# First steps of entries 4 to 7 folded about the middle row, on sixteen 32x32 tiles

## Chip, cores and metric

The kernel runs on one core of one Trainium2 chip. The metric is the time of one execution on the device in microseconds (us); the median of several runs counts. The engines of the core are named as in the profile: PE (TensorE, matmuls), PEld (its weight loads), DVE (VectorE), ACT (ScalarE), POOL (GpSimd) and SP (SyncE, which here only issues DMA transfers).

## What is computed

Eight entries of 3136 rows and 256 channels go through a global filter (a real Fourier transform along the rows, a product with a filter, the inverse), and the 25088 rows that come out go through a two-layer network with a softmax-like activation and a normalization:

```python
X = np.fft.rfft(x, axis=1)
y = np.fft.irfft(X * (filt_r + 1j * filt_i)[None], n=x.shape[1], axis=1)
h = y.reshape(B * S, D) @ w_in                      # 25088 x 256 @ 256 x 1024
e = np.exp(h - h.max(-1, keepdims=True))
solu = h * (e / (e.sum(-1, keepdims=True) + 1e-9))
mu, var = solu.mean(-1, keepdims=True), solu.var(-1, keepdims=True)
out = ((solu - mu) / np.sqrt(var + 1e-6) * g_ln) @ w_out   # 1024 -> 256
```

## The kernel before

**The transform.** 3136 = 49 x 64. An entry is a grid of 49 rows by 64 columns of 256 channels. Its transform has four parts. The *first step* is a 49-point transform down the columns; a *piece* of it takes four columns from the left and the four mirrored ones from the right, so an entry has 8 pieces. The *forward step* (`forward`, pb), the product with the filter (`multiply`, on DVE) and the *inverse step* (`inverse`, pc) work on 7 groups of an entry, "spectra". The *back transform* (`fetch_back`, `back_halves`, py, and `join_halves`, on DVE) has 8 pieces again and writes the rows `y` that the network reads. Between the parts the data go through DRAM: `d1` after the first step, `d2` after the inverse.

**The network.** Rows go in blocks of 128; 196 blocks. Two blocks make a pair, and both matrix products of a pair are done in seven products in place of eight (Strassen's way): `product(j, m)` is the first layer (m, line 799), `project(p, m)` the second (o, line 935). The sums that this needs are GpSimd's: `pair_sums` of `y` (s, line 778) and `project_sums` of the activation (u and solu_t, line 778). DVE evacuates the first layer (`finish`, lines 820 and 823), normalizes (`normalize`, line 845) and transposes (`turn`, line 863); ACT copies (`keep`, line 809), takes exponentials and squares. `regroup` (line 880) is eight transfers a pair on SP's queue, which bring the transposed activation (turn) into the layout of the second layer (solu_t). `deviations` (lines 890 to 893) is three small operations on GpSimd every fourth block.

**Steps.** The order on every engine is written out by hand. `step(k)` runs once for each block k; even and odd steps do different parts of a pair. Work of the transform is hung into steps through lists: `early`, `middle` and `late` (matmuls of the transform and joins at three places in a step; `late` is at its end), `stores`, `loads` (at the end of a step), `differences` and `products` (at its start), `first_parts` and `second_parts` (the product with the filter). In an even step after the tenth, `differences` and `products` are the first things issued; in an odd one they follow `stores`. `PLAN[e]` names for each entry the steps of its 8 pieces of the first step, its 7 spectra and its 8 back pieces. Engines issue in order, so a waiting instruction holds up all that is behind it on its engine, and a waiting transfer all transfers behind it on its queue.

**The first step of entries 2 to 7, before.** For a piece in step t, `fetch_quarters` loads a row buffer on SP's queue with four transfers: partitions 0 to 48 hold two columns and 64 to 112 the other two, each with its mirror columns beside it. In step t DVE takes the difference of columns and mirrors (line 279, into diff), GpSimd the sum in place (line 285), and in `late[t]` four matmuls of 49 rows on 64x64 tiles (line 294, each in two passes) give the four real combinations into two PSUM banks. Two ACT copies (line 299) bring them back into the row buffer, and in step t+1 two transfers of 200 KB on GpSimd's queue store them to `d1` (line 305). The table `wq_t` holds the weights.

**Row buffers.** Pool `r` has four buffers of 128 x 1024 floats. The pieces of the first step and those of the back transform (t4, loaded on GpSimd's queue, line 380) share them. `row_loads` lists all these loads with the step of their use, t; a short planner puts each into `loads[at]`:

```python
at = max(t - 3, earliest, min(row_loads[n - 4][0] + 1, latest)) if n >= 4 else -1
```

A load waits for the buffer that it is given: for a first-step piece until its store to `d1` has landed, for a back piece until its join has read it.

## Time and profile before

| | |
|---|---|
| median of 3 runs | 1569.08 us (1568.96 to 1569.52) |
| the profiled execution | 1569.28 us, span 1567.5 us, TensorE clock 0.996 |
| L935 second layer, busy | 400.2 + 309.6 us |
| L799 first layer, busy | 398.4 + 307.8 us |
| L396 py, L326 pc and pb | 64.7, 55.7 + 54.1 and 47.8 us |
| L294 pa, entries 2 to 7 | 53.5 + 52.9 us (overlapping), 590 ns each |
| L279 difference, L285 sum | 0.69 us (0.67 to 3.32), 1.28 us each |

The span is the time from the first to the last instruction of the profiled execution. Busy times of one engine's groups can overlap, since matmuls are pipelined and tiles of the array run side by side. A row of the timeline gives start, duration, engine, line, operation, what it writes and reads, how many were merged, and in brackets the idle time before it and what ended it. Steps have no marker in the trace; an even step begins with the first L799 matmul behind the last matmul of `late`.

### The profile page before, as it was taken

To read this page: it belongs to the slowest core of one execution; us is meant where nothing else is said; L and a number is where in the kernel's file an instruction comes from. 1 tells how busy PE (TensorE), PEld (TensorE's weight loads), DVE (VectorE), ACT (ScalarE), POOL (GpSimd) and SP (SyncE) were. 2 spreads that over 40 slices of the span, in tenths; PEclk is the share of its full clock that TensorE was granted. 3 is DMA by queue.
4 is the path that set the end of the run, shared out by engine and by line. 5 is a ranking of instruction groups with operands and counts; after the bars stand their busy time and mean duration, and the time that the engine had idled before them with its cause. 6 is when DMAs were issued, how large, how long until landed. Compare 5 with 4: busy or idle time off the path is not lost.

```text
span 1567.5 us, 36719 instructions
## 1 busy us (share of the span) xinstructions
PE 1532.5 (98%) x12844; PEld 1061.7 (68%) x12844; DVE 1254.9 (80%) x2233; ACT 927.9 (59%) x1898; POOL 1157.2 (74%) x1346
## 2 busy tenths in 40 slices
PE   8988999999999999999999999999999999999997
PEld 5633576667666776667766776667776777777777
DVE  4879878897998789878998698877998777776773
ACT  3565655666556656666566655666556666666663
POOL 2578886697879678887779767786766767676665
PEclk9999999999999999999999999999999999999999
DMA  9768788877987689667886588766874545343434
GB/s 246 252 202 226 218 225 220 227 212 207 252 242 204 173 236 254 196 173 192 249 230 190 152 229 247 203 184 176 233 204 119 138 122 135 88 115 102 116 104 118
DMA packets 342256, 298.07 MB, mean 190 GB/s; under 512 B 27915, under 2 KB 311573, under 8 KB 342073
## 3 DMA queue, kind: packets, MB, share of 16 engines
q1 hardware_dynamic: 278872, 175.82, 42.5%
q0 software_dynamic: 29568, 87.33, 18.6%
q10 hardware_dynamic: 33634, 32.58, 7.2%
q8 instruction: 104, 1.70, 0.5%
q14 instruction: 78, 0.64, 0.1%
HBM read 118.02 MB, written 74.84 MB: 123 GB/s over the span
## 4 chain that ended last, share of the span: by engine, by line
PE 59%; DMA 2%; DVE 0%; SPq 0%; issue 0%; POOL 0%; ACT 0%; ACTq 0%; POOLq 0%
PE o L935 26%; PE m L799 26%; PE py L396 2%; PE pc L326 1%; PE pa L294 1%; PE pb L326 1%; DMA solu_t<-turn 1%; DMA x<-in_x_dram 0%; SPq L880 0%; DMA out_dram<-ot 0%; PE o L899 0%; POOL u L778 0%; ACT e L833 0%; DVE h L845 0%; DVE h L820 0%
## 5 line engine op out<-in xcount | busy, mean ns | idle before, releaser
L935 PEld LDWEIGHTS o<-w_out_sb,solu_t 128*128 128x128 f32 x3136 | 381.1, 192 | 47.3 <-issue 43.5
L799 PE MATMUL m<-w_in_sb,s 128*128 128x512 f32 x784 | 398.4, 609 | 5.8 <-ACT h L809 3.3
L935 PE MATMUL o<-w_out_sb,solu_t 128*128 128x128 f32 x3136 | 400.2, 276 | 1.7 <-DVE ot L955 1.6
L935 PEld LDWEIGHTS o<-w_out_sb,u 128*128 128x128 f32 x2352 | 306.4, 191 | 138.3 <-issue 108.6
L799 PE MATMUL m<-w_in_sb,y 128*128 128x512 f32 x588 | 307.8, 607 | 5.6 <-DVE nmax L823 3.8
L935 PE MATMUL o<-w_out_sb,u 128*128 128x128 f32 x2352 | 309.6, 275 | 2.6 <-POOL u L778 1.8
L845 DVE SCALAR_TENSOR_TENSOR h<-e,h 128x1024 f32<-128x1024 f32 x196 | 308.7, 1575 | 0.4 <-ACT e L833 0.4
L951 ACT ACTIVATE ot<-o,rs_t 128x128 f32<-128x128 f32 x392 | 143.6, 367 | 248.2 <-PE o L935 246.1
L809 ACT COPY h<-m 128x512 f32<-128x512 f32 x294 | 173.2, 589 | 195.6 <-PE m L799 191.0
L778 POOL TENSOR_TENSOR u<-solu_t 128x512 f32<-128x512 f32 x98 | 135.0, 1377 | 184.7 <-DMA solu_t<-turn 126.2
L823 DVE CUSTOM_DVE_ANT_0 h<-m,h 128x512 f32<-128x512 f32 x196 | 134.3, 685 | 165.4 <-ACT h L809 103.1
L853 ACT ACTIVATE h<-h,nmu 128x1024 f32<-128x1024 f32 x196 | 225.1, 1148 | 53.4 <-DVE turn L863 53.4
L863 DVE STREAM_TRANSPOSE turn<-h 128x1024 f32<-128x1024 f32 x196 | 243.0, 1240 | 3.8 <-DVE ot L955 0.3
L833 ACT ACTIVATE e<-h,nmax 128x1024 f32<-128x1024 f32 x196 | 225.3, 1149 | 8.1 <-DVE h L845 6.6
L778 POOL TENSOR_TENSOR u<-solu_t,u 128x512 f32<-128x512 f32 x98 | 136.0, 1388 | 94.0 <-PE o L935 93.4
L799 PEld LDWEIGHTS m<-w_in_sb,s 128*128 128x128 f32 x784 | 127.9, 191 | 90.9 <-issue 71.6
L955 DVE SCALAR_TENSOR_TENSOR ot<-o,rs_t,ot 128x128 f32<-128x128 f32 x299 | 103.7, 347 | 97.0 <-ACT ot L951 59.8
L778 POOL TENSOR_TENSOR u<-u,solu_t 128x512 f32<-128x512 f32 x98 | 161.9, 1652 | 15.9 <-PE o L935 9.0
L799 PEld LDWEIGHTS m<-w_in_sb,y 128*128 128x128 f32 x588 | 96.7, 191 | 102.1 <-issue 46.2
L778 POOL TENSOR_TENSOR solu_t<-solu_t,solu_t 128x512 f32<-128x512 f32 x98 | 155.0, 1581 | 0.9
L778 POOL TENSOR_TENSOR s<-y 128x128 f32<-128x128 f32 x196 | 100.2, 511 | 6.1 <-DMA x<-in_x_dram 5.7
L396 PEld LDWEIGHTS py<-wb_t,t 50*64 50x64 f32 x3584 | 57.6, 135 | 42.9 <-issue 18.7
(121 smaller groups left out, 1953.9 us busy)
## 6 DMA issues: line engine op xcount, KB each, us to landing
solu_t<-turn SPq DMA_DIRECT2D x780, 128.0 KB
out_dram<-ot SPq DMA_DIRECT2D x196, 128.0 KB
t<-d POOLq DMA_DIRECT2D x112, 200.0 KB, 6.8
d<-x POOLq DMA_DIRECT2D x100, 200.0 KB, 5.3
t<-d ACTq DMA_DIRECT2D x37, 512.0 KB
f<-f_dram POOLq DMA_DIRECT2D x37, 512.0 KB, 7.6
d<-g POOLq DMA_DIRECT2D x36, 512.0 KB, 5.0
x<-in_x_dram SPq DMA_DIRECT2D x112, 98.0 KB
```

The costliest lines, as they stand in the source:

```text
L396: nc.tensor.matmul(out=views[g][64 * h:64 * h + 64, cb, i, :], lhsT=t4[rows, i, c0:c0 + 64], rhs=wb_t[rows, 0:N1], start=True, stop=True)
L778: nc.gpsimd.tensor_tensor(out=out, in0=in0, in1=in1, op=op)
L799: nc.tensor.matmul(out=ms[j, bank], lhsT=lhsT, rhs=w_in_sb[:, w, :], start=m in (1, 2, 7), stop=True, skip_group_check=True)
L809: nc.scalar.copy(out=h_half(k, i), in_=ms[j, 0])
L823: nc.vector.tensor_tensor_reduce(out=h_half(k, i), in0=ms[j, bank], in1=h_half(*kept), scale=1.0, scalar=sofar, op0=ALU.add, op1=ALU.min, ...
L833: nc.scalar.activation(out=e, in_=hs[k], func=AFT.Exp, bias=nmaxs.pop(k)[:, 1:2], scale=-1.0, accum_out=esums[g][:, i:i + 1])
L845: nc.vector.scalar_tensor_tensor(out=solu, in0=e, scalar=SHRINK, in1=solu, op0=ALU.mult, op1=ALU.mult, accum_out=nmu)
L853: nc.scalar.activation(out=solu, in_=solu, func=AFT.Square, bias=nmu, scale=-float(DFF), accum_out=variances[g][:, i:i + 1])
L863: nc.vector.transpose(out=turns[g][:, :, i, :], in_=solus[k].rearrange("p (f j) -> p f j", j=32))
L935: nc.tensor.matmul(out=pos[p, bank], lhsT=lhs[:, f, :], rhs=w[:, f, :], start=f == 0 and (m in (1, 2, 7) or alone), stop=True, skip_group_ ...
L951: nc.scalar.activation(out=out_half(p, *to)[0], in_=pos[p, 0], func=AFT.Copy, scale=rs)
L955: nc.vector.scalar_tensor_tensor(out=ot, in0=pos[p, bank], scalar=rs, in1=out_half(p, *kept)[0], op0=ALU.mult, op1=ALU.add)
```

## The change

For entries 4 to 7 (`FOLD = 4`) the first step is folded a second time, about the middle row of the 49: sums and differences of row r and row 48 - r leave combinations of 25 rows. The four combinations need weights of 25 x 25, which stand in a new table `wz` of four 32x32 tiles; it is loaded into the buffer of `wq_t` once entry 3 is done. Two pieces are done at once.

- **Loads.** For rows in mirrored order, 256 KB pieces of x are copied from DRAM to DRAM: `turn_rows` (8 steps ahead), then `mirror_rows` twice (7 and 5 steps ahead, the second from what `turn_rows` wrote). `fetch_folded` then loads two row buffers with two transfers each. All seven transfers of a pair of pieces are on SP's queue, in place of eight. The loads go into `row_loads` with t - 1 as their step.
- **Arithmetic.** In steps t-1 and t: `difference_folded` (DVE) and `sum_folded` (GpSimd), each on 128 x 512, then `fold`, four DVE operations on 128 x 256, in `middle`.
- **Matmuls.** In `late[t]`: 16 matmuls of 25 rows on 32x32 tiles, into four PSUM banks: two that first steps and back transforms use, and the two of the forward and inverse steps. Four ACT copies bring them back.
- **Stores.** In step t+1, one transfer of 512 KB for each of the two pieces on GpSimd's queue; `d1` has 32 rows in place of 25 for these entries.
- **Plan.** The pairs of pieces stand in every fourth step, the first five spectra in every fourth step between them (then every second), back pieces in every second. Entry 3's first steps move from 15, 23, 25 ... 35 to 15, 17 ... 29; its spectra are spread too.

```diff
-    ([15, 23, 25, 27, 29, 31, 33, 35], range(38, 52, 2), range(54, 70, 2)),
-    (range(39, 55, 2), range(58, 72, 2), range(76, 92, 2)),
-    (range(63, 79, 2), range(82, 96, 2), range(100, 116, 2)),
-    (range(87, 103, 2), range(106, 120, 2), range(126, 142, 2)),
-    (range(111, 127, 2), range(130, 144, 2), range(150, 166, 2)),
+    (range(15, 31, 2), [32, 36, 40, 44, 48, 50, 52], range(56, 72, 2)),
+    *((range(24 * e - 61, 24 * e - 45, 4), [24 * e - n for n in (40, 36, 32, 28, 24, 22, 20)],
+       range(24 * e - 16, 24 * e, 2)) for e in range(4, 8)),
...
-    ph = 2 * np.pi * (np.outer(n1, s) % N1) / N1
+    ph = 2 * np.pi * (np.outer(n1 - NS + 1, s) % N1) / N1
...
+    wz = np.zeros((32, 4, 32))
+    for a, table in enumerate((w[0], w[1], w[1], -w[0])):
+        wz[:NS, a, :NS] = table[:NS]
+    wz[NS - 1] /= 2
...
-    d1 = [dram.tile([NS, P, C], FP32, name=f"d1_{e}") for e in range(B)]
+    d1 = [dram.tile([NS if e < FOLD else 32, P, C], FP32, name=f"d1_{e}") for e in range(B)]
...
+        def rows_of(self, i, half, mirror):
+            n2 = N2 - 4 * i - 8 if mirror else 4 * i
+            n1, row = ((0, N2 * C), (N1 - 1, -N2 * C))[half]
+            return x[self.e].offset + (n1 * N2 + n2) * C, row
+
+        def turn_rows(self, i, half, dma):
+            at, row = self.rows_of(i, 1, True)
+            self.turned[i, half] = out = dram.tile([4, 32, 2 * C], FP32, name=f"turned_{self.e}_{i}_{half}")
+            dma(out=out, in_=bass.AP(tensor=x.tensor, offset=at, ap=[[2 * C, 4], [row, 32], [1, 2 * C]]))
+
+        def mirror_rows(self, i, half, dma):
+            self.mirrored[i, half] = out = dram.tile([4, 32, 2 * C], FP32, name=f"mirrored_{self.e}_{i}_{half}")
+            if half == 0:
+                at, row = self.rows_of(i, 0, True)
+                rows = bass.AP(tensor=x.tensor, offset=at + 6 * C, ap=[[row, 32], [-2 * C, 4], [1, 2 * C]])
+            else:
+                rows = self.turned.pop((i, half)).rearrange("a r c -> r a c")[:, ::-1, :]
+            dma(out=out.rearrange("a r c -> r a c"), in_=rows)
+
+        def fetch_folded(self, i, mirror, dma):
+            self.xs[i + mirror] = out = self.pools["r"].tile([P, NCH, C], FP32, ..., tag="r")
+            for half in range(2):
+                if mirror:
+                    rows = self.mirrored.pop((i, half)).rearrange("a r c -> (a r) c")
+                else:
+                    at, row = self.rows_of(i, half, False)
+                    rows = bass.AP(tensor=x.tensor, offset=at, ap=[[2 * C, 4], [row, 32], [1, 2 * C]])
+                dma(out=out[:, 2 * half:2 * half + 2, :].rearrange("p n c -> p (n c)"), in_=rows)
+
+        def folded(self, i, n):
+            return [self.xs[i + m].rearrange("p (h n) c -> p h n c", h=2)[:, :, (n, 1 - n)[m]] for m in range(2)]
+
+        def difference_folded(self, i, n):
+            x0, x1 = self.folded(i, n)
+            self.diffs[i + n] = diff = self.pools["diff"].tile([P, 2, C], FP32, ..., tag="diff")
+            nc.vector.tensor_tensor(out=diff, in0=x1, in1=x0, op=ALU.subtract)
+
+        def sum_folded(self, i, n):
+            x0, x1 = self.folded(i, n)
+            nc.gpsimd.tensor_tensor(out=x0, in0=x0, in1=x1, op=ALU.add)
+
+        def fold(self, i, n):
+            (x0, x1), diff = self.folded(i, n), self.diffs.pop(i + n)
+            for out, in0, in1, op in ((x1[:, 0], x0[:, 0], x0[:, 1], ALU.subtract),
+                                      (x0[:, 0], x0[:, 0], x0[:, 1], ALU.add),
+                                      (x1[:, 1], diff[:, 0], diff[:, 1], ALU.subtract),
+                                      (x0[:, 1], diff[:, 0], diff[:, 1], ALU.add)):
+                nc.vector.tensor_tensor(out=out, in0=in0, in1=in1, op=op)
+
+        def first_folded(self, i, pss):
+            for a, (m, half) in enumerate(((0, 0), (1, 1), (1, 0), (0, 1))):
+                data = self.xs[i + m][:, 2 * half:2 * half + 2, :][:, ::1 - 2 * m]
+                for g in range(4):
+                    rows = slice(32 * g, 32 * g + NS)
+                    nc.tensor.matmul(out=pss[g][32 * a:32 * a + 32], lhsT=wq_t[rows, a], rhs=data[rows],
+                                     start=True, stop=True)
+            for g in range(4):
+                nc.scalar.copy(out=self.xs[i + g // 2][:, 2 * (g % 2):2 * (g % 2) + 2, :], in_=pss[g])
+
+        def store_folded(self, i, dma):
+            dma(out=d1[self.e].rearrange("s (a n) c -> a s n c", a=4)[:, :, NCH * i:NCH * i + NCH, :],
+                in_=self.xs.pop(i))
...
+            elif e >= FOLD:
+                for by, job in ((8, lambda dma, sp=sp, i=i: sp.turn_rows(2 * i, 1, dma)),
+                                (7, lambda dma, sp=sp, i=i: sp.mirror_rows(2 * i, 0, dma)),
+                                (5, lambda dma, sp=sp, i=i: sp.mirror_rows(2 * i, 1, dma))):
+                    loads[t - by].append(lambda job=job: job(nc.sync.dma_start))
+                for n in range(2):
+                    row_loads.append((t - 1, t - 2, -1, lambda sp=sp, i=i, n=n: sp.fetch_folded(
+                        2 * i, n, nc.sync.dma_start)))
+                    differences[t - 1 + n].append(lambda sp=sp, i=i, n=n: sp.difference_folded(2 * i, n))
+                    products[t - 1 + n].append(lambda sp=sp, i=i, n=n: sp.sum_folded(2 * i, n))
+                    middle[t - 1 + n].append(lambda sp=sp, i=i, n=n: sp.fold(2 * i, n))
+                    stores[t + 1].append(lambda sp=sp, i=i, n=n, dma=dma: sp.store_folded(2 * i + n, dma))
+                late[t].append(lambda sp=sp, i=i: sp.first_folded(
+                    2 * i, [psum(f"pa_{sp.e}_{i}_{g}") for g in range(2)] + psum_pair(f"pa_{sp.e}_{i}", False)))
...
+        if k == PLAN[FOLD - 1][0][-1] + 1:
+            nc.gpsimd.dma_start(out=wq_t, in_=wz_dram)
```

More of the change, by code (lines that the diff above doesn't have):

```diff
@@ L36 @@
 EARLY = 3
+FOLD = 4
 PLAN = [
@@ L104, in dft_tables @@
     return wf.reshape(NR, NK).astype(f32), wf0.astype(f32), wq.reshape(P, 2, 64).astype(f32), \
+        np.tile(wz, (4, 1, 1)).astype(f32), \
         (-wi0).reshape(P, NR).astype(f32), (-wb).reshape(P, N1).astype(f32), de.astype(f32)
@@ L120 @@
     nc = tc.nc
-    wf_host, wf0_host, wq_host, wi_host, wb_host, de_host = dft_tables()
+    wf_host, wf0_host, wq_host, wz_host, wi_host, wb_host, de_host = dft_tables()
     wf_dram = nc.inline_tensor(wf_host, name="wf_tbl").ap()
@@ L124 @@
     wq_dram = nc.inline_tensor(wq_host, name="wq_tbl").ap()
+    wz_dram = nc.inline_tensor(wz_host, name="wz_tbl").ap()
     wi_dram = nc.inline_tensor(wi_host, name="wi_tbl").ap()
@@ L149 @@
     wf_t = consts.tile([NR, NK], FP32, name="wf_t")
-    wq_t = consts.tile([P, 2, 64], FP32, name="wq_t")
+    wq_t = consts.tile([P, 4, 32], FP32, name="wq_t")
+    wq_halves = wq_t.rearrange("p (j b) i -> p j (b i)", j=2)
     wi_t = consts.tile([P, NR], FP32, name="wi_t")
@@ L219, in __init__ @@
             self.units = [(i, min(2, NP - i)) for i in range(0, NP, 2)]
+            self.turned, self.mirrored = {}, {}
             self.xs, self.t1s, self.t2s, self.fs, self.prods, self.gs, self.des, self.spectra, self.diffs = (
@@ L294, in first_quarters @@
                     nc.tensor.matmul(out=pss[g][64 * j:64 * j + rows],
-                                     lhsT=wq_t[64 * g:64 * g + N1, j, 0:rows],
+                                     lhsT=wq_halves[64 * g:64 * g + N1, j, 0:rows],
                                      rhs=rhs[64 * g:64 * g + N1], start=True, stop=True)
@@ new lines, in fetch_folded @@
+        def fetch_folded(self, i, mirror, dma):
+            self.xs[i + mirror] = out = self.pools["r"].tile([P, NCH, C], FP32, name=f"x_{self.e}_{i + mirror}",
+                                                             tag="r")
+            for half in range(2):
[5 more added lines that the diff above has]
+                dma(out=out[:, 2 * half:2 * half + 2, :].rearrange("p n c -> p (n c)"), in_=rows)
@@ new lines, in folded @@
+        def folded(self, i, n):
+            return [self.xs[i + m].rearrange("p (h n) c -> p h n c", h=2)[:, :, (n, 1 - n)[m]] for m in range(2)]
+        def difference_folded(self, i, n):
+            x0, x1 = self.folded(i, n)
+            self.diffs[i + n] = diff = self.pools["diff"].tile([P, 2, C], FP32, name=f"diff_{self.e}_{i + n}",
+                                                               tag="diff")
+            nc.vector.tensor_tensor(out=diff, in0=x1, in1=x0, op=ALU.subtract)
@@ L581 @@
             load_w_out(n, nc.sync.dma_start)
-        nc.sync.dma_start(out=wq_t, in_=wq_dram)
+        nc.sync.dma_start(out=wq_halves, in_=wq_dram)
         nc.sync.dma_start(out=wb_t[:, 0:N1], in_=wb_dram)
@@ L1043 @@
         at = max(t - 3, earliest, min(row_loads[n - 4][0] + 1, latest)) if n >= 4 else -1
+        import os
+        if os.environ.get('DBG'): print(n, t, at, latest, row_loads[n-4][0])
         assert at < t
```

## Prediction

> **What bounds the kernel now.** I read the page's first, second and fourth part, then the engines by stretch, then the order of instructions on TensorE, GpSimd and VectorE in steps of the stage that changes. Page:
>
> ```profile
> PE 1532.5 (98%) x12844; PEld 1061.7 (68%) x12844; DVE 1254.9 (80%) x2233; ACT 927.9 (59%) x1898; POOL 1157.2 (74%) x1346
> PEclk9999999999999999999999999999999999999999
> PE 59%; DMA 2%; DVE 0%; SPq 0%; issue 0%; POOL 0%; ACT 0%; ACTq 0%; POOLq 0%
> ```
>
> TensorE is busy 98% of the span at full clock, and the chain that ended last is TensorE almost alone. So a matmul taken away is time won, and any wait put in front of TensorE is time lost: it has no idle time to absorb one. By stretch (length, busy time of PE, PEld, DVE, ACT, POOL, clock, DMA share, GB/s):
>
> ```profile
> 740.00:920.00 180.00, 180.00 (x1619) 125.13 (x1621) 151.87 (x267) 109.51 (x227) 142.18 (x167) 1.00 0.75 208
> ```
>
> In this stage VectorE (152 of 180) and GpSimd (142) keep up, with little room. TensorE at the end of step 97 and the start of step 98:
>
> ```profile
> 847.30 1.06 PE L935 MATMUL o<-w_out_sb,solu_t 128*128 128x128 f32 x8
> 848.29 0.65 PE L294 MATMUL pa<-x,wq_t 49*64 49x512 f32 x2
> 848.30 0.64 PE L294 MATMUL pa<-diff,wq_t 49*50 49x512 f32 x2
> 848.77 0.59 PE L294 MATMUL pa<-x,wq_t 49*64 49x512 f32 x1
> 849.29 1.12 PE L799 MATMUL m<-w_in_sb,y 128*128 128x512 f32 x2
> 850.26 1.05 PE L935 MATMUL o<-w_out_sb,u 128*128 128x128 f32 x8
> ```
>
> A piece's first step is four 64x64 tiles, each in two passes: all first passes start within 0.01 us, the second ones 0.47 later, and the next projection 1.00 us after the first start. Eight L935 matmuls elsewhere take 0.89 and two L799 0.86; here they take 0.99 and 0.97. So a piece that stands alone costs 1.00 + 0.10 + 0.11 = 1.21 us. Where it follows an inverse step (770.61, next projection 771.60; the last inverse matmuls start at 770.42 and stream 0.21), that switch is paid already and it costs twice 0.43 = 0.87. GpSimd in steps 86 and 87 (they begin at 755.04 and 763.46):
>
> ```profile
> 756.45 1.28 POOL L778 TENSOR_TENSOR u<-solu_t 128x512 f32<-128x512 f32 x1 [5.19 <-DMA solu_t<-turn]
> 757.82 1.28 POOL L778 TENSOR_TENSOR u<-u,solu_t 128x512 f32<-128x512 f32 x1
> 759.03 0.80 POOL L371 DMA_DIRECT2D d<-g  x1
> 759.86 1.45 POOL L778 TENSOR_TENSOR solu_t<-solu_t,solu_t 128x512 f32<-128x512 f32 x1
> 762.01 1.27 POOL L778 TENSOR_TENSOR u<-solu_t,u 128x512 f32<-128x512 f32 x1 [0.70 <-PE o L935]
> 763.24 0.65 POOL L890 TENSOR_TENSOR rs<-var,floor 128x4 f32<-128x4 f32 x1
> ...
> 765.58 0.80 POOL L713 DMA_DIRECT2D f<-f_dram  x1
> 766.40 1.29 POOL L285 TENSOR_TENSOR x<-x 113x512 f32<-113x512 f32 x1
> ```
>
> The chain is in order: projection sums, store, sums, deviations, filter load, and only then the sum of a piece; 10.5 us from 756.45 to 767.69 without the 0.70 for TensorE. It ends 4.2 us into the odd step, and nothing but that step's last matmuls (6.2 us in) needs it. VectorE in step 97 (842.05 to 849.29) and at the end of step 109 (936.66):
>
> ```profile
> 845.22 1.24 DVE L863 STREAM_TRANSPOSE turn<-h 128x1024 f32<-128x1024 f32 x1
> 846.37 0.71 DVE L820 TENSOR_SCALAR_CACHE_REDUCE h<-m,nmax 128x512 f32<-128x512 f32 x1
> ...
> 936.93 1.22 DVE L845 SCALAR_TENSOR_TENSOR h<-e,h 128x1024 f32<-128x1024 f32 x1
> ```
>
> VectorE's L820 clears the PSUM bank that the projection at 849.29 writes; it ends at 847.08, 2.2 us early. The normalization of an odd step ends 1.5 us inside the next even one (938.15).
>
> **The change, part by part.** *TensorE.* Before, entries 4 to 7 have 32 pieces; by the plan 22 stand in a step with an inverse and 10 alone: 22 x 0.87 + 10 x 1.21 = 31.2 us. After, 16 groups of 16 tiles, all alone, two pieces each. The trace has no 32x32 tile. Bounds: all 16 at once, 1.21 us, or one column of four after another, 4 x 0.87 + 0.34 = 3.8. The four tiles shown run at once, 0.01 to 0.03 apart, so I take 1.21 plus 0.14 for 16 starts: 16 x 1.35 = 21.6, a gain of 9.6. The new plan spreads the spectra over every fourth step: forward steps that share a step with a back transform fall from 27 to 19, each giving up about one switch, 0.34 us: +2.8. With one more shared piece in entry 3, TensorE gains 7.
>
> *VectorE.* The difference stays (0.69, L279's median). Added are four 128x256 operations a piece, 128. Nearest row: L349 on 64x256, 417 ns; 512 wide it is 0.69 to 2.78 when GpSimd runs beside it. I take 1.5 us for the four (bounds 1.4 and 3.3). A pair adds 3 us to two steps in which VectorE was idle 4 to 5 us with a back transform alone: hidden as work. Its place is not: each piece's fold waits for GpSimd's sum, stands ahead of the transpose and of L820, and the tiles wait for all of it.
>
> *GpSimd.* Now the two sums stand in steps t-1 and t, the first at the head of the even step's queue, ahead of the projection sums; it waits for VectorE's difference, which stands behind the normalization: 1.5 + 0.69 + 1.28 = 3.5 us into the step before the projection sums begin (756.45 was 1.4 in). Then the chain above, 10.5 us, to the second sum's end: 14.0. An even step with a back transform alone lasts 7.5 (877.72 to 885.22), so that is 6.5 into the odd step; plus the fold, 8.0. The tiles could start at 6.24 (848.29 - 842.05): 1.8 late. The transpose and L820 follow (845.22 to 847.08, 1.9) and end at 9.9, where the next projection would stand at 9.0: 0.9 more. **2.7 us a pair**, from 1.2 (a normalization that ends at 0.7 and no slow operation in the chain) to 5.
>
> *SP and the buffers.* The four row buffers now hold two pieces for four steps. The loads of 12 of the 16 pairs (the first pair of each entry has free buffers) are issued at the end of step t-4, while by the buffers that the program gives them they wait for a back transform's join and for the store of the piece before, both in step t-3. SP stands, and behind it the regrouping transfers that GpSimd sums at step t-1. The store is queued as before, 3.5 us into step t-3 (d<-x at 775.10, step 88 from 771.60), and lands 5.0 later (512 KB, d<-g in the page's issues; 6.8 for t<-d): with 8.6 us a step, at the end of t-3. Then two issues of about 0.6 (L880's median 0.63), 5.0 to land, 6.7 into t-2; SP's transfers take eight landing semaphores in turn, so the second half of the regrouping waits for that; three more issues, 8.6; step t-2 lasts 7.3; 3.8 us to land (128 KB on GpSimd's queue): 5.1 us into step t-1. So the projection sums start at 5.1 in place of 3.5 (bounds: 3.5, and 7.1 with 6.8 for the store): **4.3 us a pair** in place of 2.7.
>
> SP's issues fall from 144 to 112, and 48 of them copy 256 KB from DRAM to DRAM, 12.6 MB; loads and 32-row stores add 5.7 to the 298 MB. At a DMA share of 0.75 this lengthens the landings above, inside their bounds. ScalarE copies as often as before, four in a row, 2.4 us in place of 1.2; its first result that TensorE waits for is due 3.7 us later, so that is hidden. Entry 3 moves to steps 15 to 29, among eight back transforms in steps 16 to 22 that already run long: 0 to 6 us, taken as 2. The second table's load is one transfer.
>
> **Sum.** 1569.3 (span 1567.5 with 1.8 around it; the median of the runs is 1569.1) - 7 + 4 x 2.7 + 12 x 4.3 + 2 = 1626.7, say 1626 us. With 1.2 us for every pair it would be 1581; with 6.3 and 5 for the two kinds, 4 less gain and 6 for entry 3, 1667.
>
> **Rivals.** *Faster: the sums come in time.* If GpSimd's second sum ends by 4.5 us into the odd step, as 767.69 does now, the fold ends when the tiles could start, and only TensorE's 7 us are left: 1562. For it: TensorE waits for GpSimd 1.8 us in the whole trace at L935, and VectorE's stretch of step 97 has 2.2 us to spare. Against it: the two sums and the difference ahead of a 10.5 us chain that already ends at 4.2.
>
> *VectorE alone.* The folds stretch beside GpSimd's operations to their upper bound, 3.3 us a piece, and the sums come in time: 1.8 us late a pair and 0.5 at the even fold, 16 x 2.3 - 7: 1599. For it: L279 takes 0.67 to 3.32 us. Against it: 4 to 5 us of idle VectorE in steps with a back transform alone.
>
> *The tiles do not run at once.* Then a pair costs 3.8 in place of 1.35: 39 us on top of the forecast, 1665. In the trace two column halves of one row group start 0.01 us apart in both passes, which speaks against it. The Trainium skill, "TensorE: Matmul & The Clock Gate", Part 3 on packing, says that a weight load overlaps running matmuls only where the row group differs; by that rule the four columns of one row group would follow each other, and this time would be the one. The trace shows the second pass's weights of both halves loaded under the first pass, so I give it little.
>
> **How the numbers follow.** Forecast 0.63; faster 0.17; VectorE alone 0.10; tiles in turn 0.04; a balance of gain and small waits that ends within 0.2% (3 us, about what a measurement of this kernel tells from no change) 0.06. Predicted: 1626. The forecast's own range is 1585 to 1655; down to 1565 it takes in the VectorE case and the even one, and leaves out most of the faster case and the tiles in turn. Faster 0.17, same 0.06, slower 0.77.
>
> **What would show it.** Right: TensorE's idle time or its waits name the folds (through GpSimd's sum) in odd steps, some 3 to 5 us, every fourth step from 35 to 119, less in steps 35, 59, 83 and 107; VectorE's folds wait for GpSimd, GpSimd's projection sums for landings of solu_t<-turn, SP's loads of x for the join and for d<-x. The 16 tiles start within 0.3 us. Wrong: a two-step length near 14.9 in fold steps (12.4 bare, 1.3 back transform, 1.35 tiles), or waits of TensorE for ScalarE's copies.

## The result, and the profile after

The changed kernel takes 1844.7 us (median of 4 runs, 1842.0 to 1848.4), the kernel before 1569.3 in the same comparison: 1.1745 times as long (95% interval 1.1708 to 1.1782). The prediction had the sign, but 57 us where there were 275. The page of the changed kernel, in the parts that were shown of the kernel before:

```profile
PE 1613.6 (88%) x13100; PEld 1105.6 (60%) x13100; DVE 1320.3 (72%) x2361; ACT 926.4 (50%) x1898; POOL 1133.4 (62%) x1315
PEclk9999989998879899898989899899999999999999
PE 49%; DMA 27%; POOL 9%; issue 5%; DVE 5%; SPq 3%; ACT 1%; POOLq 0%; ACTq 0%; DVEq 0%
```

Two things can be read from it. TensorE is idle 226.5 us (1840.1 - 1613.6) in place of 35.0, and the chain that ended last, which was TensorE almost alone, now goes through transfers for 27% of the span. And TensorE is busy 81 us longer than before although it should have less to do: the mean granted clock fell from 0.996 to 0.942, which is 107 us of full clock lost (0.058 x 1840) in place of 6 (0.004 x 1567). Of the 107, 78 fell into time in which TensorE was busy (before: 5), summed over the trace; the others fell into its idle time and cost nothing. So the span of the profiled execution is 273 us longer, of which 191 are idle time, 73 are clock, and some 8 neither.

Where the time went is seen step by step. I took each two steps from the start of one even step to the next, and subtracted what the prediction's figures give for a step pair without any wait (12.4 us, and 0.9 to 1.3 for each visit of the transform). What is left I call the rest of a step pair; a table at the end of the experiments has these rests for several kernels. For the kernel before they add up to 6 us over the whole run (single ones reach 1.5 us, so a rest of that size says nothing), for the changed kernel to 289, of which 277 in these places: 12.8 us for each of the 12 pairs of pieces whose loads wait for buffers, the "held pairs" (154 in all); 4.9 for each of the other four; 60 in the steps just ahead of an entry's first spectrum (54, 56, 78, 80, 102, 104, 128); 25 behind each entry's last pair of pieces; 18 in steps 20 and 30.

One pair, that of step 63, shows how the 12.8 come about. SP's queue, GpSimd's, VectorE's and TensorE's rows of the changed kernel (step 62 begins at 674.5, step 63 at 689.2, step 64 at 704.8):

```profile
665.75 1.17 SPq L341 DMA_DIRECT2D x<-in_x_dram  x2
679.10 0.80 SPq L341 DMA_DIRECT2D x<-mirrored  x2
679.95 5.55 SPq L960 DMA_DIRECT2D solu_t<-turn  x8
```

```profile
665.75 1.47 POOL L378 DMA_DIRECT2D d<-x  x2
...
681.47 1.12 POOL L460 DMA_DIRECT2D t<-d  x2 [9.54 <-DMA d<-x]
683.68 1.27 POOL L355 TENSOR_TENSOR x<-x,x 128x512 f32<-128x512 f32 x1 [1.09 <-DVE diff L351]
690.75 1.27 POOL L858 TENSOR_TENSOR u<-solu_t 128x512 f32<-128x512 f32 x1 [5.80 <-DMA solu_t<-turn]
...
699.17 1.27 POOL L355 TENSOR_TENSOR x<-x,x 128x512 f32<-128x512 f32 x1
```

```profile
682.85 0.69 DVE L351 TENSOR_TENSOR diff<-x,x 128x512 f32<-128x512 f32 x1 [6.76 <-DMA x<-mirrored]
...
700.48 1.26 DVE L364 TENSOR_TENSOR x<-x 128x256 f32<-128x256 f32 x2 [5.18 <-POOL x L355]
```

```profile
679.34 1.05 PE L1015 MATMUL o<-w_out_sb,u 128*128 128x128 f32 x8
685.61 2.08 PE L1015 MATMUL o<-w_out_sb,solu_t 128*128 128x128 f32 x8 [5.21 <-DVE ot L1035]
687.48 3.58 PE L879 MATMUL m<-w_in_sb,s 128*128 128x512 f32 x4
...
701.99 2.92 PE L372 MATMUL pa<-x,wq_t 25*32 25x512 f32 x32 [4.90 <-DVE x L364]
```

The two stores of the pair before were issued at 665.75 (GpSimd's line 378). SP's second load stands from 666.9 to 679.1 until a store has landed, GpSimd's load for a back transform until 681.47, and the regrouping comes behind SP's load. VectorE's difference waits 6.76 us for the late piece; what is behind it on VectorE (line 1035, the output's sums) is late, and TensorE waits for that. Then the projection sums wait for the regrouping until 690.75, the second sum follows 8.4 us later, the fold behind that, and the tiles behind the fold. This is the chain that the prediction described, but the store holds it for 13 us, not 5, and TensorE stops twice. After the first stop the four matmuls at 687.48 take 3.58; at a clock of 1.00 four of this line take 1.88 (at 845.24 of the same trace). By stretch (length, busy time of PE, PEld, DVE, ACT and POOL, then granted clock, DMA share, GB/s):

```profile
676.00:686.00 10.00, 4.79 (x83) 3.31 (x82) 3.24 (x8) 3.66 (x8) 2.39 (x3) 0.90 0.72 200
686.00:694.00 8.00, 8.00 (x32) 5.20 (x31) 4.63 (x12) 1.44 (x3) 3.18 (x3) 0.69 0.88 214
```

In the 8 us behind the stop TensorE is busy throughout, and its clock is 0.69.

### The profile page after: what moved, and what is told of

The parts are those of the page before. It is cut to its first block, busy times and chain, and to the rows that moved or that the text cites. A ratio compares the mean times of both kernels' runs of the same rounds, so it can differ in the third digit from the quotient of the medians.

```text
span 1840.1 us, 37177 instructions
## 1 busy us (share of the span) xinstructions
PE 1613.6 (88%) x13100; PEld 1105.6 (60%) x13100; DVE 1320.3 (72%) x2361; ACT 926.4 (50%) x1898; POOL 1133.4 (62%) x1315
## 4 chain that ended last, share of the span: by engine, by line
PE 49%; DMA 27%; POOL 9%; issue 5%; DVE 5%; SPq 3%; ACT 1%; POOLq 0%; ACTq 0%; DVEq 0%
PE o L1015 20%; PE m L879 20%; DMA solu_t<-turn 7%; DMA d<-x 6%; DMA de<-de_tbl 4%; DMA t<-d 4%; POOL u L858 3%; DMA x<-mirrored 2%; PE pb L406 2%; PE py L476 2%; DMA x<-in_x_dram 2%; DVE x L364 2%; SPq L960 2%; PE pc L406 2%; POOL solu_t L858 1%
## 5 line engine op out<-in xcount | busy, mean ns | idle before, releaser
L1015 PE MATMUL o<-w_out_sb,solu_t 128*128 128x128 f32 x3136 | 419.9, 283 | 86.6 <-DVE ot L1035 85.7
L1015 PEld LDWEIGHTS o<-w_out_sb,solu_t 128*128 128x128 f32 x3136 | 397.1, 198 | 139.7 <-DVE ot L1035 90.7
L879 PE MATMUL m<-w_in_sb,s 128*128 128x512 f32 x784 | 421.2, 640 | 23.9 <-ACT h L889 14.9
L1015 PEld LDWEIGHTS o<-w_out_sb,u 128*128 128x128 f32 x2352 | 316.0, 197 | 165.0 <-issue 134.6
L1015 PE MATMUL o<-w_out_sb,u 128*128 128x128 f32 x2352 | 318.0, 280 | 18.9 <-ACT ot L1031 17.3
L879 PE MATMUL m<-w_in_sb,y 128*128 128x512 f32 x588 | 320.0, 628 | 11.9 <-DVE h L900 6.7
L858 POOL TENSOR_TENSOR u<-solu_t 128x512 f32<-128x512 f32 x98 | 132.8, 1355 | 269.8 <-DMA solu_t<-turn 213.8
L925 DVE SCALAR_TENSOR_TENSOR h<-e,h 128x1024 f32<-128x1024 f32 x196 | 287.8, 1468 | 0.4 <-ACT e L913 0.4
L879 PEld LDWEIGHTS m<-w_in_sb,s 128*128 128x128 f32 x784 | 133.7, 200 | 112.3 <-issue 84.5
L858 POOL TENSOR_TENSOR solu_t<-solu_t,solu_t 128x512 f32<-128x512 f32 x98 | 149.3, 1523 | 1.2
L355 POOL TENSOR_TENSOR x<-x,x 128x512 f32<-128x512 f32 x32 | 40.8, 1274 | 112.4 <-DVE diff L351 72.3
## 6 DMA issues: line engine op xcount, KB each, us to landing
d<-x POOLq DMA_DIRECT2D x32, 512.0 KB, 13.2
```

Source lines behind the costliest of these rows:

```text
L858: nc.gpsimd.tensor_tensor(out=out, in0=in0, in1=in1, op=op)
L879: nc.tensor.matmul(out=ms[j, bank], lhsT=lhsT, rhs=w_in_sb[:, w, :], start=m in (1, 2, 7), stop=True, skip_group_check=True)
L925: nc.vector.scalar_tensor_tensor(out=solu, in0=e, scalar=SHRINK, in1=solu, op0=ALU.mult, op1=ALU.mult, accum_out=nmu)
L1015: nc.tensor.matmul(out=pos[p, bank], lhsT=lhs[:, f, :], rhs=w[:, f, :], start=f == 0 and (m in (1, 2, 7) or alone), stop=True, skip_group_ ...
```

## The experiments

Each is one execution beside one of the kernel before on the same chip (1571 to 1578 there). Four runs of the changed kernel lay 6 us apart, so a difference under that says nothing.

**What makes a store land in 13 us?** GpSimd's transfers to `d1` and `d2` by issuer, with size and median time to landing, first in the kernel before, then in the changed kernel:

```profile
d<-x POOLq DMA_DIRECT2D x100, 200.0 KB, 5.3
d<-g POOLq DMA_DIRECT2D x36, 512.0 KB, 5.0
```

```profile
d<-g POOLq DMA_DIRECT2D x36, 512.0 KB, 4.9
d<-x POOLq DMA_DIRECT2D x32, 512.0 KB, 13.2
```

What was under way while SP's copy `turned` (line 318, issued at 659.84) ran alone on SP's queue (q1), from 664 to 665.7, and then on GpSimd's queue (q0) while the two stores issued at 665.75 were under way, from 668 to 676:

```profile
DMA packets 91, 0.17 MB, mean 101 GB/s; under 512 B 4, under 2 KB 10, under 8 KB 91
q1 hardware_dynamic: 91, 0.17, 26.2%
```

```profile
q0 software_dynamic: 352, 0.79, 38.7%
```

Two transfers of 512 KB from the same queue, one in 4.9 us and one in 13.2. In the 1.7 us from 664 on only the copy runs, and it keeps 26.2% of 16 engines busy: 4.2 engines. The two stores together keep 38.7% busy: 6.2 engines, some 3 each. The slowest dimension of the copy's source is 4 (`[[2 * C, 4], [row, 32], [1, 2 * C]]`); so is that of the new stores in `d1` and of the loads of x. The old store had 50 there. The Trainium skill, "DMA: Bandwidth & Descriptors", section "Why a DMA increments its semaphore by 16 and not by 1", says that a transfer runs on the largest number of engines, up to 16, that divides the slowest dimension of both of its sides. By that rule these have 4 engines, and for the copy the trace agrees with its 4.2; for a store the 3 are an average over two that ran at once.

The first experiment gives the stores a slowest dimension of 32:

```diff
-            dma(out=d1[self.e].rearrange("s (a n) c -> a s n c", a=4)[:, :, NCH * i:NCH * i + NCH, :],
-                in_=self.xs.pop(i))
+            xi, rows = self.xs.pop(i), d1[self.e].rearrange("s (a n) c -> a s n c", a=4)
+            for a in range(4):
+                dma(out=rows[a, :, NCH * i:NCH * i + NCH, :], in_=xi[32 * a:32 * a + 32])
```

> Each store of a folded piece is four transfers of 32 partitions (128 KB) in place of one whose slowest dimension is 4. Theory A (a transfer with a slowest dimension of 4 runs on a few of the 16 DMA engines; the 13.2 us landing of the stores is what holds SP): a store's parts land in 4 to 7 us, SP's wait for them falls from 108 us to under 30, and the time falls to 1680 to 1730. Theory B (the place of the loads: SP stands ahead of the regrouping whatever the landing): the time stays above 1790. Theory C (GpSimd's chain and the sums' order set the fold): above 1800, and GpSimd's six further issues a pair (about 3 us) make it slower still.

1786.9 us. The parts land in 3.2 us, and SP's wait for d<-x falls from 108.4 to 45.4, not below 30:

```profile
d<-x POOLq DMA_DIRECT2D x128, 128.0 KB, 3.2
```

The 25 us behind the last pairs are gone, and a held pair costs 10.4 in place of 12.8. The direction is A's, but a third to a half of the amount: something else holds the pairs as well. Whether it is shape or size that made them quick, a second split tells, into four transfers of 128 KB that keep the slowest dimension of 4:

```diff
+            xi, rows = self.xs.pop(i), d1[self.e].rearrange("s (a n) c -> a s n c", a=4)
+            for n in range(NCH):
+                dma(out=rows[:, :, NCH * i + n, :], in_=xi[:, n, :])
```

> The changed kernel, with each store of a folded piece in four transfers of one column (128 KB), each still with a slowest dimension of 4 in d1. It tells whether the four transfers of 32 partitions were quicker for their shape or for their size. Theory A (shape: few DMA engines): they land in 9 us or more, and the time stays above 1830 (also for six more issues on GpSimd). Rival (size): they land in under 6 us and the time falls to about 1787, as with the four of 32 partitions.

```profile
d<-x POOLq DMA_DIRECT2D x128, 128.0 KB, 7.1
```

1826.2 us. The same number and size of transfers takes more than twice as long to land and saves 18 us in place of 58. So most of the gain is the shape's; the smaller size may have a part, since both landing (7.1) and time lie between the two forecasts.

**The loads of x, and their place.** Each load with a slowest dimension of 4 becomes four of 32 rows:

```diff
+                    for a in range(4):
+                        dma(out=out[32 * a:32 * a + 32, 2 * half:2 * half + 2, :].rearrange("p n c -> p (n c)"),
+                            in_=bass.AP(tensor=x.tensor, offset=at + 2 * C * a + (31 * row if half else 0),
+                                        ap=[[abs(row), 32], [1, 2 * C]]))
+                    continue
```

> The loads of x are four transfers of 32 rows each in place of one with a slowest dimension of 4; rows 17 to 48 are read in rising order, which changes the values of entries 4 to 7 and nothing else. Stores stay as in the changed kernel. Theory A: the loads land sooner by themselves, but the stores still hold SP: 1800 to 1850. Theory A2 (the loads of x, not the stores, are what comes late): VectorE's wait for x (72 us) goes, and the time falls to 1730 to 1780. Theory B: as now, 1840 to 1870, since SP issues six more transfers a pair (4 us).

> Stores in four transfers of 32 partitions and loads of x in four of 32 rows each (rows 17 to 48 in rising order: the values of entries 4 to 7 change, nothing else), so that no store and no load of x has a slowest dimension of 4. Theory A (few DMA engines for such transfers, and the loads matter as soon as the stores are quick): in place of the 1787 of the stores alone, 1690 to 1730; what stays is the 70 us in the steps 54 to 59, 78 to 83, 102 to 107 and 128. Theory B (place of the loads ahead of the regrouping): 1770 to 1800.

The loads alone: 1865.0 us, 20 more, with SP's six further issues a pair and the stores still in the way. That is in B's range, 15 above A's, and against A2. Both: 1750.6, so behind quick stores the quick loads are worth 36 us. A held pair is at 7.4. The time is 20 us above what A expected and 20 below what B did, so neither is the whole.

The place of the loads, one step later (`at = t - 2` in the planner for these loads, which is step t-3 of the pair), once with slow transfers and once with quick ones:

```diff
+        if at >= 0 and latest == t - 1 and earliest == -1 and t > 20:
+            at = t - 2
```

> Stores and loads as in the changed kernel; the loads of x of entries 4 to 7 stand one step later on SP's queue (end of step t-3), behind the regrouping of that step. Theory B: SP is no longer in front of the regrouping, GpSimd's wait for solu_t falls from 214 us to near the 126 of the kernel before, and the time falls to 1650 to 1700. Theory A: the store still lands late, so the loads do, and VectorE's difference waits for them: the time stays between 1780 and 1860, with the wait moved from GpSimd (solu_t) to VectorE (x<-mirrored).

> As the kernel with both edits, and the loads of x one step later, behind the regrouping of step t-3. Theory A: the late place was bad (1912 in place of 1845) because stores and loads were slow; with quick ones SP stands free for the regrouping and the time is 10 to 40 us below that of both edits alone. Theory B: the same direction, but 60 us or more. If VectorE's difference still waits for x (over 60 us in the waits), the late place loses again.

1912.1 and 1789.3 us: 67 and 39 more than with the early place. Neither theory had the first (A ended at 1860), and for the second both had expected a gain, unless VectorE still waits for x; it does, 84.7 us. Of the first, the waits of VectorE and GpSimd:

```profile
DVE diff L351 <- DMA x<-mirrored: 180.4, 16, 15.5
POOL u L858 <- DMA solu_t<-turn: 137.5, 32, 16.8
```

The wait moved, as A said: GpSimd's for the regrouping falls from 213.8 to 137.5, VectorE's for x rises from 72.4 to 180.4. So in these two kernels SP's place ahead of the regrouping (B) is not by itself what costs; x is late either way.

**The landing semaphores.** SP's waits in the changed kernel, and in the kernel before the row of its regrouping (line 880):

```profile
SPq L341 <- DMA d<-x: 108.4, 12, 26.7
SPq L341 <- DVE y L490: 86.0, 11, 10.7
SPq L328 <- DMA t<-d: 82.4, 12, 11.2
SPq L960 <- DMA t<-d: 77.3, 13, 15.4
```

```profile
SPq L880 <- DMA t<-d: 11.3, 4, 6.7
```

The first two are the prediction's. The last two it did not have: neither the copies (328) nor the regrouping (960) reads t, the spectrum's rows, which ScalarE loads. The changed kernel's timeline shows it, SP's queue first, then ScalarE's (step 52 begins at 579.7, step 54 at 593.7):

```profile
577.49 26.13 SPq L960 DMA_DIRECT2D solu_t<-turn  x8
```

```profile
598.46 0.38 ACTq L396 DMA_DIRECT2D t<-d  x1
598.88 0.53 ACTq L839 DMA_DIRECT2D de<-de_tbl  x1
```

Eight regrouping transfers, which otherwise take some 5.5 us to issue, take 26.13. In the built program the transfers of both queues count their landings on eight semaphores, dealt out in one order, and a transfer waits until the last user of its semaphore has landed. The seventh and eighth of these transfers were given the semaphores of the two transfers that ScalarE issues at 598.46 and 598.88, in its place in step 54. They wait for something that stands later in the order of the work. The program has 19 such cases, the kernel before 2. In the trace SP stands in ten cases, 107 us in all, ahead of a transfer while the last user of its semaphore has not yet been issued by ScalarE; in the kernel before in one, 6.7 us. The remedy puts the spectra's loads of entries 3 to 7 on SP's own queue:

```diff
-            dma = nc.sync.dma_start if e == 1 and t < 8 else nc.scalar.dma_start
+            dma = nc.sync.dma_start if e >= 3 or e == 1 and t < 8 else nc.scalar.dma_start
...
+        if sp.e >= 3:
+            dma = nc.sync.dma_start
```

> The changed kernel, with the spectra's loads of d1 and of the table de (entries 3 to 7) on SP's queue in place of ScalarE's; stores and loads of x as they are. Theory D (SP's and ScalarE's transfers share eight landing semaphores in one order; in the new plan 19 of SP's transfers in place of 2 are given the semaphore of a transfer that stands later on ScalarE, and wait until that one is issued and lands): the 70 us in steps 54 to 59, 78 to 83, 102 to 107 and 128 go, SP's waits for t<-d (160 us) fall below 30, and the time falls by 60 to 90, to 1755 to 1785. Against D: those steps stay as long, the time 1830 to 1860.

> Stores and loads split as above (values of entries 4 to 7 change) and the spectra's loads on SP's queue. Theories A and D together: the two savings add up, 1600 to 1660, near the 1626 of the prediction, whose working took the stores as 5 us and did not know of the semaphores. If the sum is not reached (above 1700), a third cause (GpSimd's chain and the sums' order, or the clock) holds the rest.

Alone: 1768.4 us, 76 less. The 60 us ahead of the first spectra become 10, the 6.6 of step 30 nothing, and SP's waits for t<-d 32:

```profile
SPq L962 <- DMA t<-d: 32.0, 18, 6.2
```

D holds: in this kernel SP stands so in one case, 6.3 us. With stores and loads split: 1696.9. Of the two savings (94 and 76) 148 us are had together. The time lies above the 1600 to 1660 that A and D expected of both, and 126 us against the kernel before stay.

**What is left.** First the sums of the folded pieces on VectorE (`nc.vector` in place of `nc.gpsimd`, just ahead of `fold`), then the loads right behind the regrouping of step t-3, each on top of the one before:

```diff
-            nc.gpsimd.tensor_tensor(out=x0, in0=x0, in1=x1, op=ALU.add)
+            nc.vector.tensor_tensor(out=x0, in0=x0, in1=x1, op=ALU.add)
...
-                    products[t - 1 + n].append(lambda sp=sp, i=i, n=n: sp.sum_folded(2 * i, n))
+                    middle[t - 1 + n].append(lambda sp=sp, i=i, n=n: sp.sum_folded(2 * i, n))
```

```diff
+            for job in mid_loads[k]:
+                job()
             if 0 <= j - 4 < pairs:
                 project_sums(j - 4, 1)
```

> The kernel with split stores and loads and the spectra's loads on SP's queue (values of entries 4 to 7 change by the row order of one load), and the sums of the folded pieces on VectorE, just ahead of the fold, in place of GpSimd. Theory E (the prediction's own: what is left, about 5 us a pair, is GpSimd's second sum behind the projection sums, and the first ahead of them): 40 to 70 us less than 1697, so 1625 to 1660. Theory F (what is left is late loads of x and of the back transforms): within 15 us of 1697, or slower, since VectorE has more to do.

> As the kernel with the sums on VectorE, and the loads of x stand right behind the regrouping of step t-3 (ahead of the output's stores) in place of the end of step t-4. Theory F: another 20 to 50 us less than with the sums alone. Theory E: within 10 us of it.

1684.6 and 1661.4 us. Moving the sums is worth 12, not 40 to 70, and a held pair's rest stays (6.7 for 6.6): GpSimd's chain is a small part of what is left, or what it gives VectorE's added sums take back; this run does not separate the two. The place of the loads is worth 23 when all is quick, as F expected. Both gains are mostly clock: its mean goes from 0.965 to 0.972 and 0.984, and what it takes while TensorE is busy from 47 to 38 and 22 us.

Entry 3, whose pieces stand among entry 1's back transforms (in step 21 of the changed kernel TensorE waits 6.42 and 1.79 us for t, the back transform's rows), moved in two ways:

```diff
-    (range(15, 31, 2), [32, 36, 40, 44, 48, 50, 52], range(56, 72, 2)),
+    ([15, 17, 23, 25, 27, 29, 31, 33], [36, 38, 40, 44, 48, 50, 52], range(56, 72, 2)),
```

> As the kernel with the sums on VectorE, with entry 3's pieces at steps 15, 17, 23, 25 ... 33 in place of 15, 17, 19 ... 29, and its second spectrum at 38 with the first at 36. If the 11 to 16 us lost in steps 20 and 21 come from entry 3's loads among entry 1's back transforms: 8 to 14 us less than with the sums alone. If they come from the back transforms and the other queues: no change, or a few us more for the step in which an inverse step and the 16 tiles meet.

> All of these but the later loads, with the right values: rows 48 to 17 of the first piece come through one more copy from DRAM to DRAM (256 KB a pair), which gives its load a slowest dimension of 128. It should lie within 10 us of the kernel with entry 3's pieces moved; each further us is the price of the copy, which itself still runs with a slowest dimension of 4.

1694.6, 10 more than without the move: steps 20 and 21 give 9 us, and steps 34 to 47 take 11 back. The kernel with the extra copy takes 1670.2, 24 less than the one without, where at most 10 either way were expected. The copy makes one transfer of four loads, so SP has fewer issues and the load another shape; which of these outweighs the copy, no run separates. So all loads went through copies, without the move of entry 3 and then with a third place for its pieces (15, 17, 23 to 27 and 29), on top of the loads behind the regrouping:

> Right values: the kernel with the sums on VectorE and the loads of x behind the regrouping, where all rows come through copies in DRAM (two more of 256 KB a pair), so that the four loads of a pair are four transfers with a slowest dimension of 128 in place of ten. Theory F (what is left, some 90 us, is x that comes late, and SP's time for its issues): less than the 1661 of that kernel, 1625 to 1655. Rival (what is left does not hang on the loads): 1655 to 1675, by two more copies on SP's queue.

> As the kernel with all rows through copies, with entry 3's pieces at steps 15, 17, 23, 24, 25, 26, 27 and 29, so that its spectra stay at 32 and later. If entry 3's loads among entry 1's back transforms cost 11 us in steps 20 and 21: 8 to 12 us less. The rival is that other steps give it back, as they did with the pieces at 31 and 33: no gain.

1653.4 us, at the upper end of F's range but only 2 us outside its rival's, which decides nothing, and 1637.4, 16 less by entry 3's place (8 to 12 were expected). The last is 207 us quicker than the changed kernel and 64 slower than the kernel before. VectorE's folds of the two pieces in step 71 (it begins at 681.6) of that kernel:

```profile
682.52 0.89 DVE L367 TENSOR_TENSOR x<-x 128x256 f32<-128x256 f32 x2
683.32 0.75 DVE L367 TENSOR_TENSOR x<-diff 128x256 f32<-128x256 f32 x2
...
686.69 1.16 DVE L367 TENSOR_TENSOR x<-x 128x256 f32<-128x256 f32 x2
687.77 2.90 DVE L367 TENSOR_TENSOR x<-diff 128x256 f32<-128x256 f32 x2
690.59 1.23 DVE L949 STREAM_TRANSPOSE turn<-h 128x1024 f32<-128x1024 f32 x1
```

The first piece's fold takes 1.6 us, the second's, beside GpSimd's projection sums, 4.0, and the transpose and all that TensorE needs next stand behind it. It is the only one of this kernel's 32 folds above 2.4 us, so it does not explain what its other held pairs still cost; that stays open. In the changed kernel slow folds are the rule: all 16 second folds take 2.4 us (2.44 in the rows of step 63 above, beside GpSimd's 128x128 sums `s`), and 11 of the 16 first ones 3.7 to 6.2, beside its 128x512 sums.

**The clock.** The kernel before, with TensorE held on purpose: idle GpSimd operations ahead of the projection sums of ten steps.

```diff
+        for _ in range(STALLS.get(k, 0)):
+            nc.gpsimd.tensor_tensor(out=idle_t, in0=idle_t, in1=idle_t, op=ALU.mult)
```

> The kernel before, with 8, 12, 16, 24 and 36 added GpSimd operations (128x128, on an unused tile, about 0.45 us each) ahead of the projection sums of two even steps each (60 and 72, 84 and 96, 108 and 120, 132 and 144, 156 and 168), which hold TensorE for up to about 3, 5, 7, 11 and 16 us, less the slack there. Theory G (a hold of more than some 3 us is followed by TensorE's clock at 0.5 for 3.4 us or more, so that it costs more than its length): the stretch of each longer hold shows a granted clock under 1 and loses 1.5 to 4 us on top of TensorE's idle time; the total is 40 to 70 us above the kernel before. Against G: clock 1.00 throughout, and each hold costs its idle time alone.

1619.8 us, 47 more. The stretches of one step pair each with 12, 16 and 36 operations (0.40 us each); the third line is the 11.3 us behind the one with 16:

```profile
840.60:856.50 15.90, 14.13 (x83) 9.58 (x81) 11.92 (x21) 8.93 (x19) 15.02 (x20) 1.00 0.55 158
1029.20:1048.70 19.50, 15.30 (x83) 9.58 (x81) 11.73 (x21) 8.93 (x19) 18.23 (x28) 0.92 0.58 162
1048.70:1060.00 11.30, 11.30 (x55) 8.08 (x53) 4.43 (x11) 7.10 (x14) 9.04 (x10) 0.84 0.40 104
1302.50:1326.70 24.20, 15.66 (x138) 11.63 (x137) 11.30 (x22) 8.90 (x20) 21.53 (x40) 0.83 0.27 72
```

With 12 operations in step 96 TensorE is idle 1.8 us and the clock stays at 1.00. With 16 in step 120 it is idle 4.2, and the clock is 0.92 there and 0.84 in the 11.3 us behind, in which TensorE never stops. So a stop is followed by a low clock while the work goes on, as G said. Four of the ten holds have one (steps 120, 132, 156 and 168, idle 4.1 us or more), the six others (idle 2.9 us or less) stay at 1.00. Of the 47 us some 39 are idle time of TensorE (74.0 us in place of 35.0) and some 7 clock (12 us lost while it is busy, in place of 5). How long a stop must be, TensorE's own rows of this kernel tell in part:

```profile
1044.26 1.16 PE L936 MATMUL o<-w_out_sb,solu_t 128*128 128x128 f32 x8 [2.52 <-POOL solu_t L779]
1046.70 1.19 PE L295 MATMUL pa<-x,wq_t 49*64 49x512 f32 x2 [1.28 <-POOL x L286]
...
1137.81 2.07 PE L936 MATMUL o<-w_out_sb,u 128*128 128x128 f32 x8 [4.00 <-POOL u L779]
...
1232.71 1.16 PE L936 MATMUL o<-w_out_sb,u 128*128 128x128 f32 x8 [1.80 <-POOL u L779]
```

Behind the 4.00 eight matmuls take 2.07, behind the 1.80 they take 1.16. The stop of 2.52 ends at 1044.26, and from 1045.58 to 1052.41 the granted clock is 0.50; it begins 0.2 us into the second stop, of 1.28, which is too short to have brought it about alone.

The kernels side by side. The columns after the clock are the rests described above, in us: for each of the 12 held pairs, for each of the other four, in the seven steps ahead of the first spectra, in steps 20 and 30, and behind the last pairs.

| kernel | time | clock | held pair | other pair | first spectra | 20, 30 | behind |
|---|---|---|---|---|---|---|---|
| changed | 1844.7 | 0.942 | 12.8 | 4.9 | 60 | 18 | 25 |
| stores split | 1786.9 | 0.951 | 10.4 | 4.9 | 58 | 18 | -2 |
| stores and loads split | 1750.6 | 0.959 | 7.4 | 4.5 | 58 | 21 | -2 |
| spectra's loads on SP | 1768.4 | 0.956 | 10.8 | 7.0 | 10 | 11 | 27 |
| all three | 1696.9 | 0.965 | 6.6 | 6.4 | 13 | 14 | 2 |
| and sums, later loads | 1661.4 | 0.984 | 4.5 | 4.7 | 5 | 14 | 1 |
| and copies, entry 3 | 1637.4 | 0.991 | 2.8 | 4.3 | 5 | 2 | 2 |

## Why the prediction was wrong, point by point

**The tiles: right where nothing is waited for.** Sixteen tiles in two passes, and the next projection behind them:

```profile
395.65 1.14 PE L372 MATMUL pa<-x,wq_t 25*32 25x512 f32 x32
396.72 1.13 PE L879 MATMUL m<-w_in_sb,y 128*128 128x512 f32 x2
```

1.07 us from start to start, where 1.35 was forecast. Three more of the 16 groups take 1.2; the other twelve take 2.2 to 2.9, because they stand behind a stop at a low clock (2.92 at 701.99 above) or stop in their middle for the fold. Where nothing is waited for, the 16 tiles start within 0.1 us, so the rival of tiles in turn falls; the 3.8 us a pair, which it added up from the trace and set beside the rule on packing of the Trainium skill, "TensorE: Matmul & The Clock Gate", Part 3, are not seen. TensorE's weight loads wait for ScalarE's copies (line 375) 10.9 us in the whole run. The gain of 7 us is not seen: less what the clock took, TensorE is busy 1535 us (1613.6 - 78) in place of 1527. What the many stops add to its busy time, no run separates.

**The step that failed: "SP and the buffers", by the size of its landings.** The mechanism is there as described: SP waits for d<-x and for the join, the regrouping stands behind, the sums and the fold are late. But the store was taken to land in 5.0 us, from another transfer of 512 KB, with 6.8 as the bound. It took 13.2. The loads of x behind it were given 5.0 as well; those with a slowest dimension of 4 took 10.9 (median from the issue to the last update of their semaphore in the trace). The rows behind these figures (d<-g and t<-d) had another shape than the new transfers, and the diff shows the shape; a bound from them was no bound here. Held pairs cost 12.8 in place of 4.3, which is 102 of the missing 218 us. The stores alone account for a part: with quick ones a held pair still costs 10.4 (and the 25 us behind the last pairs go), with quick loads as well 7.4. The 3.1 that stay above the forecast fall with the later edits, together with the clock; no run divides them further.

**Missing: the shared semaphores.** The prediction used that SP's transfers take eight of them in turn, but not that ScalarE's share them, and that a new order of the spectra changes who waits for whom. 60 us ahead of the first spectra and 7 in step 30, shown by the move to SP's queue (76 in all) and by SP's ten waits for transfers that ScalarE had not yet issued.

**Missing: the clock.** Every stall was costed at its length. While TensorE was busy, the low clock took 73 us more than in the kernel before; this is not a cause beside the others but a factor on them, contained in the 12.8, the 60 and the rest. The kernel before with TensorE held on purpose shows that a long stop by itself brings it about.

**Entry 3: 2 us taken, 0 to 6 allowed; 11 in steps 20 and 21.** The move of its pieces shows it: 12.6 there without, 3.3 with it.

**GpSimd's second sum, and VectorE's fold.** 2.7 us a pair was forecast for the chain ahead of the fold. At 58, 82 and 106, where no buffer is waited for, the pair cost 3.8. With the sums on VectorE only 12 us went. The fold was taken as 1.5 us with 3.3 as the bound; in the changed kernel the second fold of each pair took 2.4, and 11 of the 16 first ones went over the bound, up to 6.2. So what the rival "VectorE alone" priced is there too, beside the late sums and not in their place. What it costs, no run here separates, because VectorE's fold was never taken away.

**The range** ended at 1655, inside the 1667 that the prediction's own bounds gave; even these had 6.3 us for a held pair, because the bound of the landing came from rows with another shape. (The 7.1 us in them is 6.9 by the prediction's own figures, 2 us in the sum.) With the two causes taken out and the loads in a better place, the kernel takes 1637, which is near the 1626 of the forecast. That is no proof of its terms, for the edits changed more than those two.

## What to carry to other kernels

Before a landing time is taken from another row, compare the slowest dimensions of both sides of the transfer, not its bytes: a split into quarters of the partitions, 32 rows each, brought 13.2 us to 3.2, and a split of the same size that kept the dimension of 4 only to 7.1. Where two queues share landing semaphores, a new order of transfers makes new waits between things that have nothing to do with each other; look for a queue's wait on a transfer whose data it does not use. And where TensorE is 98% busy a stall can cost more than its length, since the clock can fall behind it (here behind four of ten holds, the four longest): price that before you sum.

## What the hardware showed that was not expected

A copy with a slowest dimension of 4 kept 4.2 of 16 DMA engines busy, and a store of 512 KB in that shape took 13.2 us where other 512 KB took 4.9. TensorE's granted clock was 0.84 over 11.3 us in which TensorE was busy throughout, behind stops of 2.52 and 1.28 us, and 1.00 behind one of 1.80. Behind the four long holds it stayed at 0.50 for 3.41, 6.83 or 10.24 us, one, two or three times 3.41. The Trainium skill, "TensorE: Matmul & The Clock Gate", section "What's actually happening", says that the clock halves after an idle window of about 3.4 us. The stop of 4.00 agrees with it; the one of 2.52 shows that a shorter stop can be enough, since the low clock began 0.2 us into the next. VectorE's four operations on 128x256 took together 1.6 us where GpSimd did little, 2.4 beside its 128x128 sums, and 3.7 to 6.2 where its 128x512 sums ran beside them.
